# Rearranging the attention slots of a fused attention and MoE kernel

## The chip, the core and the metric

The kernel runs on one core of a Trainium2 chip. The core has a matrix engine (TensorE, "PE" in the profile, with its weight loads shown apart as "PEld"), a vector engine (VectorE, "DVE"), a scalar engine (ScalarE, "ACT"), a general engine (GpSimd, "POOL") and a sync engine ("SP") whose queue issues most of the DMA transfers. Each engine works through its own instructions in program order and waits for the others by semaphores. The metric is the device time of one execution in microseconds (us). Three executions of the kernel before took 841.25 to 842.52 us, median 841.83 us.

## The reference, cut to what matters

```
scores = q @ k.T / 8                           # 4 batches x 8 heads, 576 x 576, head size 64
keep   = scores >= rowmax(scores) - tau
attn   = where(keep, exp(scores - rowmax), 0); attn /= rowsum(attn) + 1e-9
x      = (attn @ v) laid out as [4, 576, 512]
u      = x + mix(x)                            # mix: along the 576 rows, through rank 32 (U, V)
y      = u + relu(u @ w_ch1) @ w_ch2           # 512 -> 2048 -> 512
out    = (sigmoid(conv5(y)) * (y @ w_val)) @ w_out
```

All of it is wanted in fp32 accuracy. The weights U, V, w_ch1, w_ch2, w_val, conv_w and w_out arrive as 64-bit floats and are converted on the chip.

## The kernel before, in words

**Two parts.** Attention and the mixing run first (about the first 335 us of the profile), the dense layers after. In the dense part the matrix engine multiplies back to back; the change does not touch its code.

**Pairs, rows and slots.** Heads are handled in 16 pairs `p`. A pair has nine score tiles `i` = 0 to 8 of 128 queries by 576 keys: tile 0 holds the last 64 queries of both heads, the odd and even tiles after it belong to the first and the second head. The loop over slots (L701) has one score tile in each slot `s` = 9p + i. In the body of a slot VectorE and ScalarE work on tile `s` (row maximum "ns" L443, exponential "e" L457) and on the mask of tile `s`-1 (L468), then the functions put off by `later` run, and last the matrix engine's part is emitted: the scores of tile `s`+1 (L429) first, and then what the table of slots lists for this slot. In what follows "slot i" means the i-th slot of any period of nine.

**What stands in the slots.** A table `AT` says in which slot, counted from the first of pair `p`, each step of the pair is put; numbers over 8 fall into the next pair's slots. `trans_main` transposes the masked tile of two slots earlier (tile xm, L484), `trans_tail` its last 64 keys (xs, L501); `pv` multiplies with v (o, L527 and L538), once for the first two groups of tiles (slot 8) and once for the third (slot 12, which is slot 3 of the next period); `back` transposes the result (b, L548 and L551; slot 14, that is 5); `mix_t`, `mix_u` and `mix_ut` do the mixing (t L577, u L587, ut L597; slots 15 and 18, that is 6 and 0). `prep_T` transposes q, k and their tails for the next pair (tm, L356, and L370). What the matrix engine leaves in PSUM is read by ScalarE and VectorE in the slot after: q's high part on ScalarE (L323) and its low part on VectorE (L329), k likewise (L325, L333), xm to pt (L493), xs to pk (L515), b to ring (L557 on ScalarE, L563 on VectorE), t to t_st (L578, L579).

**Order inside a slot.** `ORDER` ranks the matrix engine's steps, `LATE_ORDER` the functions put off; equal ranks stay in the order in which they were listed, and a put-off function is listed when its step was called.

**Loads and stacks.** q, k and v of coming pairs are loaded two transfers a slot; `AT["lq"]` and `AT["lv"]` are the slots where such a list of loads is begun. `stacks` (slots 4 and 5) copies q and k of the next pair by DMA into the stacked operands `st` of the scores, `tails` (slot 4) does the same for tile 0 on POOL (bd, L401). The stacks and, from pair 4 on, the loads are issued by SP, in program order.

**Weight conversion.** The eight blocks of the first chunk of w_ch1 and w_ch2 are converted beside attention, by generators that move on by one step whenever `work.tick()` runs: in every slot below 18, and then in the slots of `CONVERT_AT`, counted modulo 18. A step is one instruction on ScalarE (L103, L122, L170), VectorE (L105, L108, L112, L116, L126, L172) or POOL (L124, L131, L172).

**PSUM.** Score tiles have two buffers. All other tiles of the matrix engine share four buffers in turn, so that a step may have to wait until the tile of four allocations earlier has been read.

Of the kernel before, what the change touches and what calls it, by code (L numbers as in the profile page):

```python
# [36 lines left out]
def attention_moe_kernel(  # L37
# [24 lines left out]
    NP = B * H // 2  # L62
# [6 lines left out]
    T = B * S  # L69
# [16 lines left out]
    u = const.tile([128, KD, T], F32, name="u")  # L86
# [90 lines left out]
    class Staged:  # L177
# [18 lines left out]


    AT = {
        "pv": (8, 12), "t": 15, "ut": 18, "u": 18, "Tq": 0, "Tk": 1, "Tt": 2, "stA": 4, "bd": 4, "stB": 5,
        "lq": 1, "lv": 5,  # L200
    }

    ORDER = {
        "mix_t": 4, "mix_u": 3, "mix_ut": 5, "next_scores": 0, "prep_T": 5, "pv": 3, "back": 2,
        "trans_main": 1, "trans_tail": 2,
    }
    LATE_ORDER = {
        "T": 1, "n": -1, "nt": -2, "o": -1, "t": 2, "u": 1, "x": -2,
    }

    CONVERT_AT = (0, 1, 4, 9, 10, 13, 16)
    work = Staged(4)

    def scope():
# [11 lines left out]
    def attention(dense_front, dense_mid, dense_back):  # L226
# [18 lines left out]
        bd = [bd_p.tile([128, 2, 128], F32R, name=f"bd{i}") for i in range(2)]  # L245
# [158 lines left out]
        def scores(p, i):  # L404
            d = st8[p]
            s = s_ps.tile([128, 2, 512], F32, tag="s", name="s")
            if i == 0:
                qk, t = d["qk"], bd[p % 2]
                ops = [(t[:, 0, :], qk[:, 1, :]), (t[:, 1, :], qk[:, 1, :]), (t[:, 0, :], qk[:, 2, :])]
            else:  # L410
                c, hh = divmod(i - 1, 2)
                c *= 128
                if p:
                    st = d["st", hh]
                    lhs = st[:, 0, c:c + 128]
                    ops = [(lhs, st[:, 1, :]), (lhs, st[:, 2, :])]
                else:
                    ops = [(d["st", hh][:, m, c:c + 128], d["qk"][:, n, :]) for m in (0, 1) for n in (1, 2)]
                    if hh:
                        for o, n, a in ((s[:, 0], TL, SM), (s[:, 0, TL:], HS - TL, 0), (s[:, 1], HS, HS - TL)):  # L420
                            for m, (lhs, rhs) in enumerate(ops):
                                nc.tensor.matmul(
                                    o[:, 0:n], lhs, rhs[:, a:a + n], start=(m == 0), stop=(m == len(ops) - 1)
                                )
                        d["s", i] = s
                        return
            for n in range(2):
                for m, (lhs, rhs) in enumerate(ops):
                    nc.tensor.matmul(  # L429
                        s[:, n, 0:HS], lhs, rhs[:, n * HS:(n + 1) * HS], start=(m == 0), stop=(m == len(ops) - 1)  # L430
                    )
            d["s", i] = s
# [174 lines left out]
        for hh in range(2):  # L607
            t = st8[0]["st", hh] = st_p.tile([128, 3, S], F32R, tag="st", name="st")
# [57 lines left out]
                nc.gpsimd.tensor_tensor(out=lo, in0=w[a:a + R, o:o + n], in1=f(lo), op=ALU.subtract)  # L666
            done.append(0)

        NS = 9 * NP + AT["u"] - 7
        slots = [[] for _ in range(NS + 1)]  # L670
        def put(s, what, *a):
            slots[s].append((what, a))

        for p in range(NP):
            s0 = 9 * p
            for i in range(9):
                put(s0 + i + 2, trans_main, p, i)
                if i % 2 == 0:
                    put(s0 + i + 2 + (i == 8), trans_tail, p, i)
            put(s0 + AT["pv"][0], pv, p, 0, 1)  # L680
            put(s0 + AT["pv"][1], pv, p, 2)
            put(s0 + AT["pv"][1] + 2, back, p)
            if p + 1 < NP:
                s1 = s0
                put(s1 + AT["Tq"], prep_T, p + 1, "q")
                put(s1 + AT["Tk"], prep_T, p + 1, "k")
                put(s1 + AT["Tt"], prep_T, p + 1, "tail")
                put(s1 + AT["stA"], stacks, p + 1, 0)
                put(s1 + AT["bd"], tails, p + 1)
                put(s1 + AT["stB"], stacks, p + 1, 1)  # L690
            put(s0 + AT["t"], mix_t, p)
            put(s0 + AT["ut"] - (p == NP - 1), mix_ut, p)
            put(s0 + AT["u"] - (p == NP - 1), mix_u, p)
        def next_scores(s):
            scores(*divmod(s + 1, 9))

# [3 lines left out]
        scores(0, 0)  # L700
        for s in range(NS):  # L701
            p, i = divmod(s, 9)
# [6 lines left out]
            def wtick(at):  # L709
                if at == 3 and (s < 18 or s % 18 in CONVERT_AT) or at == 1 and 2 <= s < 8:  # L710
                    work.tick()
# [305 lines left out]
    with tc.manual_schedule():  # L1017
        attention(dense_front(), dense_mid, dense_back)
        dense()
# [30 lines left out]
```

## Time and profile before

| what | value |
|---|---|
| time, median of 3 runs | 841.83 us |
| profiled execution, first to last instruction | 840.1 us |
| PE busy, share of the span | 820.9 us, 98% |
| PEld busy | 692.5 us, 82% |
| DVE busy | 617.3 us, 73% |
| ACT busy | 440.3 us, 52% |
| POOL busy | 239.5 us, 29% |
| PE busy from 60 to 100 us | 38.47 of 40 us |
| DVE busy from 60 to 100 us | 35.01 of 40 us |
| ACT busy from 60 to 100 us | 33.11 of 40 us |

The page of the profile gives the span of the profiled execution and no time of its own around it; the median of the timed runs is 1.73 us above that span. The busy time of PE counts matmuls whose ends are modelled and which overlap, so it hides short waits. The rows of the three stretches at the bottom of the table show that in attention VectorE and ScalarE are nearly as full as the matrix engine.

### The profile page before, as it was taken

The numbers are of one execution on the slowest core, as the hardware profiler recorded it, in microseconds if no ns is written. First come the engines' busy times: TensorE is split into PE (matmuls) and PEld (weight loads), VectorE is DVE, ScalarE is ACT, GpSimd is POOL, SyncE is SP. The second block draws the span as 40 slices with busy tenths as digits, with TensorE's granted clock in tenths as the row PEclk, the third lists the DMA queues.
The fourth block names the chain that finished last, engine by engine and source line by source line (L and its number), as shares of the span: only waits on it lengthen the run. The fifth ranks groups of instructions, "written<-read, shape, count | busy, mean of one in ns | idle before, by whom it ended". The sixth has DMA issues, their size and how long they took to land.

```text
span 840.1 us, 14282 instructions
## 1 busy us (share of the span) xinstructions
PE 820.9 (98%) x5084; PEld 692.5 (82%) x5084; DVE 617.3 (73%) x1309; ACT 440.3 (52%) x894; POOL 239.5 (29%) x329
## 2 busy tenths in 40 slices
PE   8999999999999999999999999999999999999998
PEld 7888877788888888788888888888888888888886
DVE  7988988889989987446883775357753588999740
ACT  5788888888888887422333332133322334445531
POOL 5845533533433432002340252004420143200000
PEclk9999999999999999999999999999999999999999
DMA  5766755665665551002120121002110111001112
GB/s 133 183 134 139 182 129 136 152 156 132 167 160 133 132 114 42 1 0 65 62 77 24 50 98 53 1 1 94 57 51 1 38 64 50 1 1 51 51 50 76
DMA packets 63567, 68.07 MB, mean 81 GB/s; under 512 B 43349, under 2 KB 46821, under 8 KB 63498
## 3 DMA queue, kind: packets, MB, share of 16 engines
q1 hardware_dynamic: 60730, 63.68, 29.4%
q0 software_dynamic: 1424, 3.10, 1.3%
q8 instruction: 41, 0.67, 0.3%
q10 hardware_dynamic: 1344, 0.39, 0.2%
q14 instruction: 28, 0.23, 0.1%
HBM read 35.89 MB, written 4.72 MB: 48 GB/s over the span
## 4 chain that ended last, share of the span: by engine, by line
PE 84%; ACT 6%; DVE 4%; DMA 2%; SPq 2%; issue 2%; POOL 1%; ACTq 0%; DVEq 0%; POOLq 0%
PE a L805 24%; PE c L805 24%; PE o L538 6%; PE s L429 6%; PE v L805 6%; PE p L964 6%; PE xm L484 4%; PE t L577 2%; PE o L527 2%; ACT e L457 2%; ACT pt L493 1%; DVE ns L443 1%; ACT qk L323 1%; DVE e L468 1%; DMA qn<-in_q_dram 1%
## 5 line engine op out<-in xcount | busy, mean ns | idle before, releaser
L805 PE MATMUL a<-us,w 128*128 128x512 f32 (+1 forms) x960 | 202.2, 369 | 0.0
L805 PE MATMUL c<-h,w 128*128 128x512 f32 (+1 forms) x960 | 200.8, 368 | 0.0
L805 PEld LDWEIGHTS a<-us,w 128*128 128x128 f32 x960 | 167.0, 189 | 30.9 <-DVE us L785 0.7
L805 PEld LDWEIGHTS c<-h,w 128*128 128x128 f32 x960 | 167.4, 189 | 30.0
L816 ACT ACTIVATE h<-a 128x512 fp32r<-128x512 f32 (+1 forms) x80 | 44.2, 553 | 187.5 <-PE a L805 187.3
L131 POOL TENSOR_TENSOR wf<-wf,wt 128x512 f32<-128x512 f32 (+2 forms) x43 | 57.5, 1338 | 262.9 <-DVE wt L126 262.9
L817 DVE SCALAR_TENSOR_TENSOR h<-a,h 128x512 fp32r<-128x512 f32 (+1 forms) x80 | 50.8, 636 | 103.9 <-ACT h L816 103.9
L458 POOL TENSOR_TENSOR th<-nm,tau_eff 128x1 f32<-128x1 f32 x135 | 76.8, 570 | 174.8 <-DVE ns L443 173.7
L443 DVE TENSOR_SCALAR_CACHE_REDUCE ns<-s 128x576 f32<-128x576 f32 x144 | 108.1, 751 | 20.2 <-PE s L429 19.7
L468 DVE SCALAR_TENSOR_TENSOR e<-ns,th,e 128x576 f32<-128x576 f32 x144 | 121.2, 842 | 0.5
L457 ACT ACTIVATE e<-ns,nm 128x576 f32<-128x576 f32 x144 | 111.4, 774 | 14.5 <-DVE ns L443 14.0
L429 PE MATMUL s<-st 128*128 128x288 f32 x480 | 94.4, 319 | 2.4 <-DVE ns L443 2.4
L484 PE MATMUL xm<-idn,e 128*128 128x128 f32 x576 | 87.2, 274 | 0.6 <-DVE e L468 0.3
L493 ACT ACTIVATE pt<-xm 128x512 f32<-128x512 f32 x144 | 85.3, 592 | 3.6 <-PE xm L484 0.5
L429 PEld LDWEIGHTS s<-st 128*128 128x128 f32 x480 | 67.9, 189 | 15.2 <-DVE ns L443 6.7
L484 PEld LDWEIGHTS xm<-idn,e 128*128 128x128 f32 x576 | 69.3, 141 | 3.7 <-ACT e L457 1.2
L538 PE MATMUL o<-pt,vt 128*64 128x256 f32 (+1 forms) x768 | 69.8, 331 | 0.0
L538 PEld LDWEIGHTS o<-pt,vt 128*64 128x64 f32 x768 | 41.4, 137 | 24.5 <-issue 8.3
L172 POOL TENSOR_TENSOR w<-wf,w 128x512 fp32r<-128x512 f32 x36 | 53.9, 1513 | 10.1 <-ACT w L170 10.1
L893 DVE SCALAR_TENSOR_TENSOR u<-y,cw,u 128x576 f32<-128x576 f32 x64 | 55.0, 871 | 0.6
L870 DVE TENSOR_TENSOR y<-c,y 128x64 f32<-128x64 f32 (+4 forms) x96 | 39.7, 447 | 21.3 <-PE c L805 21.3
L785 DVE TENSOR_TENSOR us<-u,us 128x1024 fp32r<-128x1024 f32 (+1 forms) x42 | 47.0, 1160 | 10.5 <-ACT us L784 10.5
(122 smaller groups left out, 1035.4 us busy)
## 6 DMA issues: line engine op xcount, KB each, us to landing
raw<-in_moe_w_ch_dram SPq DMA_DIRECT2D x32, 512.0 KB, 3.8
st<-qk SPq DMA_DIRECT2D x30, 256.0 KB, 3.9
st<-qk SPq DMA_DIRECT2D x15, 432.0 KB, 3.9
st<-qk SPq DMA_DIRECT2D x45, 144.0 KB, 4.1
out_dram<-ring SPq DMA_DIRECT2D x17, 256.0 KB, 2.0
st<-qk SPq DMA_DIRECT2D x15, 288.0 KB, 4.8
kn<-in_k_dram SPq DMA_DIRECT2D x28, 128.0 KB, 3.4
qn<-in_q_dram SPq DMA_DIRECT2D x26, 128.0 KB, 3.6
```

The costliest lines, as they stand in the source:

```text
L131: nc.gpsimd.tensor_tensor(out=dst, in0=dst, in1=tf, op=ALU.add)
L172: lo_eng.tensor_tensor(out=lo, in0=w, in1=f(hi), op=ALU.subtract)
L429: nc.tensor.matmul(s[:, n, 0:HS], lhs, rhs[:, n * HS:(n + 1) * HS], start=(m == 0), stop=(m == len(ops) - 1))
L443: nc.vector.tensor_scalar(out=ns.rearrange("p (a b) -> p a b", a=2), in0=s, scalar1=-1.0, scalar2=3.0e38, op0=ALU.mult, op1=ALU.min, accum ...
L457: nc.scalar.activation(out=row(p, i), in_=d["ns", i], func=ACTF.Exp, bias=nm[:, 0:1], scale=-1.0)
L458: (nc.gpsimd if p else nc.vector).tensor_tensor(out=th, in0=nm, in1=tau_eff, op=ALU.add)
L468: nc.vector.scalar_tensor_tensor(out=e, in0=d.pop(("ns", i)), scalar=d.pop(("th", i))[:, 0:1], in1=e, op0=ALU.is_le, op1=ALU.mult, accum_o ...
L484: nc.tensor.transpose(x[:, j * 128:(j + 1) * 128], e[:, c + j * 128:c + (j + 1) * 128], idn)
L493: later(s + 1, 0, lambda: nc.scalar.activation(out=dst, in_=x.rearrange("p (j c) -> p j c", j=4), func=ACTF.Copy), "x")
L538: nc.tensor.matmul(o, lhs, rhs, start=False, stop=stop)
L805: nc.tensor.matmul(ps[:, 0:m1], lhs, rhs, start=(m == 0), stop=(m == len(ops) - 1))
L893: nc.vector.scalar_tensor_tensor(out=g, in0=y[:, e, b, k:k + S], scalar=cw[:, k, e:e + 1], in1=g, op0=ALU.mult, op1=ALU.add)
```

## The change

Numbers in the tables of slots and ranks are changed, with three small edits of the code that reads them. From pair 2 on, the transposes of q move three slots earlier, from slot 0 to slot 6 of the period before (`Tq` -3; for pair 1 they stay in slot 0, `Tq1`). `mix_u` moves from slot 0 to slot 1, except for the last pair. `back` now comes ahead of `trans_main` in its slot, and a `trans_tail` that was listed first does too. t_st comes ahead of what else is put off with it. `tails` moves one slot later. The lists of loads begin one slot earlier. `CONVERT_AT` has five slots of 18 in place of seven.

```diff
     AT = {
-        "pv": (8, 12), "t": 15, "ut": 18, "u": 18, "Tq": 0, "Tk": 1, "Tt": 2, "stA": 4, "bd": 4, "stB": 5,
-        "lq": 1, "lv": 5,
+        "pv": (8, 12), "t": 15, "ut": 18, "u": 19, "Tq": -3, "Tk": 1, "Tt": 2, "stA": 4, "bd": 5, "stB": 5,
+        "lq": 0, "lv": 4, "Tq1": 0,
     }
     ORDER = {
         "mix_t": 4, "mix_u": 3, "mix_ut": 5, "next_scores": 0, "prep_T": 5, "pv": 3, "back": 2,
-        "trans_main": 1, "trans_tail": 2,
+        "trans_main": 2, "trans_tail": 2,
     }
     LATE_ORDER = {
-        "T": 1, "n": -1, "nt": -2, "o": -1, "t": 2, "u": 1, "x": -2,
+        "T": 1, "n": -1, "nt": -2, "o": -1, "t": 0, "u": 1, "x": -2,
     }
-    CONVERT_AT = (0, 1, 4, 9, 10, 13, 16)
+    CONVERT_AT = (0, 1, 6, 9, 16)
...
-        NS = 9 * NP + AT["u"] - 7
-        slots = [[] for _ in range(NS + 1)]
+        NS = 9 * NP + AT["ut"] - 7
+        slots = [[] for _ in range(NS + 2)]
...
             put(s0 + AT["pv"][0], pv, p, 0, 1)
+            end = p == NP - 1
...
-                put(s1 + AT["Tq"], prep_T, p + 1, "q")
+                put(s1 + AT["Tq" if p else "Tq1"], prep_T, p + 1, "q")
...
-            put(s0 + AT["ut"] - (p == NP - 1), mix_ut, p)
-            put(s0 + AT["u"] - (p == NP - 1), mix_u, p)
+            put(s0 + AT["ut"] - end, mix_ut, p)
+            put(s0 + AT["u"] - 2 * end, mix_u, p)
```

The matrix engine, slots 0 to 2 of the period in which pair 2's scores are taken, before (s is a score tile, xm and xs are transposes of a masked tile and of its tail, u and ut the mixing, tm the transposes of q or k):

```order
L587 MATMUL u<-vst,t_st_127 128x512
L589 MATMUL u<-idn,ring 128x128 x4
L597 MATMUL ut<-idn,ring 128x128
L598 MATMUL ut<-vst,t_st_127 128x64
L356 MATMUL tm<-idn,qn 128x128 x4
L429 MATMUL s<-st 128x288 x4
L484 MATMUL xm<-idn,e 128x128 x4
L356 MATMUL tm<-idn,kn 128x128 x4
L429 MATMUL s<-st 128x288 x4
L484 MATMUL xm<-idn,e 128x128 x4
L501 MATMUL xs<-idn,e 128x128
L501 MATMUL xs<-idn,e 64x128
```

The same place on the matrix engine in the changed kernel:

```order
L597 MATMUL ut<-idn,ring 128x128
L598 MATMUL ut<-vst,t_st_127 128x64
L429 MATMUL s<-st 128x288 x4
L484 MATMUL xm<-idn,e 128x128 x4
L587 MATMUL u<-vst,t_st_127 128x512
L589 MATMUL u<-idn,ring 128x128 x4
L356 MATMUL tm<-idn,kn 128x128 x4
L429 MATMUL s<-st 128x288 x4
L501 MATMUL xs<-idn,e 128x128
L484 MATMUL xm<-idn,e 128x128 x4
L501 MATMUL xs<-idn,e 64x128
```

The transposes of q have left slot 0 (they now stand behind t in slot 6), u has gone one slot down beside k, and the tail of tile 8 is transposed ahead of xm.

ScalarE, from the exponential of slot 5 to that of slot 7, before (pt and pk are the copies of xm and xs, rb and ring the result of back, t_st the mixing's first product):

```order
L457 ACTIVATE e<-ns,nm 128x576
L493 ACTIVATE pt<-xm 128x4x128
L555 ACTIVATE rb<-r 64x1
L557 ACTIVATE ring<-b_2024,r 64x64
L557 ACTIVATE ring<-b_2024,rb 64x64
L457 ACTIVATE e<-ns,nm 128x576
L493 ACTIVATE pt<-xm 128x4x128
L515 ACTIVATE pk<-xs 128x128
L578 ACTIVATE t_st_127<-t 128x128
L457 ACTIVATE e<-ns,nm 128x576
```

The same place on ScalarE in the changed kernel (buffers are numbered anew):

```order
L457 ACTIVATE e<-ns,nm 128x576
L555 ACTIVATE rb<-r 64x1
L557 ACTIVATE ring<-b_2007,r 64x64
L557 ACTIVATE ring<-b_2007,rb 64x64
L493 ACTIVATE pt<-xm 128x4x128
L457 ACTIVATE e<-ns,nm 128x576
L493 ACTIVATE pt<-xm 128x4x128
L515 ACTIVATE pk<-xs 128x128
L578 ACTIVATE t_st_127<-t 128x128
L323 ACTIVATE qk<-tm,qscale 128x512
L457 ACTIVATE e<-ns,nm 128x576
```

The three small ring instructions, which the mixing product t waits for, now come ahead of the copy pt, and q's high part (L323) has come in ahead of the exponential of slot 7.

SP's queue, one period of stacks (L383 to L391) and the load of v (vt, vk), before:

```order
L383 DMA st<-qk 64x1728
L384 DMA st<-qk 64x1152
L391 DMA st<-qk 64x576
L387 DMA st<-qk 64x576
L389 DMA st<-qk 64x2x512
L390 DMA st<-qk 64x2x64
L389 DMA st<-qk 64x2x512
L390 DMA st<-qk 64x2x64
L391 DMA st<-qk 64x576
L290 DMA vt_130<-in_v_dram 128x2x256
L296 DMA vk_132<-in_v_dram 64x64 x2
```

The same period in the changed kernel:

```order
L383 DMA st<-qk 64x1728
L384 DMA st<-qk 64x1152
L391 DMA st<-qk 64x576
L290 DMA vt_130<-in_v_dram 128x2x256
L296 DMA vk_132<-in_v_dram 64x64
L387 DMA st<-qk 64x576
L389 DMA st<-qk 64x2x512
L390 DMA st<-qk 64x2x64
L389 DMA st<-qk 64x2x512
L390 DMA st<-qk 64x2x64
L391 DMA st<-qk 64x576
L296 DMA vk_132<-in_v_dram 64x64
```

The load of vt and one vk now stands between the first head's stack and the second head's.

## Rows read from the trace of the kernel before

**Rows 1.** The page's first line.
```profile
span 840.1 us, 14282 instructions
```

**Rows 2.** The chain that ended last, by time: start, length, engine, line, count.
```profile
45.27 1.38 PE t L577 x10
...
291.15 1.35 PE t L577 x10
310.53 1.38 PE t L577 x10
```

**Rows 3.** Waits of PE from 20 to 345 us: total us, times, longest.
```profile
PE o L527 <- ACT pk L515: 4.5, 6, 1.1
PE s L429 <- DVE ns L443: 2.4, 5, 0.8
PE t L577 <- DVE ring L563: 1.9, 4, 0.5
PE t L577 <- ACT ring L557: 1.5, 4, 0.5
```

**Rows 4.** Waits of the weight loads (PEld), same stretch and columns.
```profile
PEld o L527 <- ACT pk L515: 8.5, 16, 1.4
...
PEld t L577 <- ACT ring L557: 6.8, 14, 0.8
PEld s L429 <- DVE ns L443: 6.7, 13, 1.0
```

**Rows 5.** Timeline at a slot 3: start, length, engine, instruction, [idle before <- releaser].
```profile
140.13 0.60 ACT L493 ACTIVATE pt<-xm 128x512 f32<-128x512 f32 x1
...
140.61 0.29 ACT L515 ACTIVATE pk<-xs 128x128 f32<-128x128 f32 x1
...
140.95 0.70 PE L527 MATMUL o<-pk,vk 128*128 128x256 f32 x2 [1.14 <-ACT pk L515]
```

**Rows 6.** Timeline at slots 4 to 6 of the same period.
```profile
143.51 2.57 POOL L124 TENSOR_TENSOR wt<-raw,wt 128x512 f32<-128x512 f32 x2
...
144.97 1.73 DVE L468 SCALAR_TENSOR_TENSOR e<-ns,th,e 128x576 f32<-128x576 f32 x1
...
147.31 0.68 DVE L563 TENSOR_TENSOR ring<-b,r 128x512 f32<-128x512 f32 x1
...
148.14 0.57 PE L577 MATMUL t<-ring,u 128*128 128x128 f32 x3 [0.55 <-DVE ring L563]
```

**Rows 7.** Instructions of DVE by shape, 20 to 335 us: busy, mean ns | idle before.
```profile
L443 DVE TENSOR_SCALAR_CACHE_REDUCE ns<-s 128x576 f32<-128x576 f32 x140 | 105.1, 751 | 20.2 <-PE s L429 19.7
...
L329 DVE SCALAR_TENSOR_TENSOR qk<-tm,qscale,qk 128x512 fp32r<-128x512 f32 x14 | 10.5, 751 | 13.3 <-ACT qk L323 13.1
...
L126 DVE SCALAR_TENSOR_TENSOR wt<-raw,wt 128x512 f32<-128x512 uint32 x5 | 3.4, 674 | 0.0
```

**Rows 8.** Timeline, slots 8 and 9 of one period, with q's copy behind them.
```profile
108.50 0.60 ACT L493 ACTIVATE pt<-xm 128x512 f32<-128x512 f32 x1
...
109.64 0.82 PE L527 MATMUL o<-pk,vk 128*128 128x64 f32 x4
...
113.57 0.76 DVE L443 TENSOR_SCALAR_CACHE_REDUCE ns<-s 128x576 f32<-128x576 f32 x1 [1.83 <-PE s L429]
...
115.99 0.73 ACT L323 ACTIVATE qk<-tm,qscale 128x512 fp32r<-128x512 f32 x1
```

**Rows 9.** Last stack transfer of one period, v's load, its landing, the scores using it.
```profile
129.16 0.71 SPq L391 DMA_DIRECT2D st<-qk  x1
129.96 0.74 SPq L290 DMA_DIRECT2D vt<-in_v_dram  x1
...
DMA to landing us min/median/max: 4.2/4.2/4.2
...
135.79 0.78 PE L429 MATMUL s<-st 128*128 128x288 f32 x4
```

**Rows 10.** Timeline where the dense layers begin.
```profile
336.25 0.69 DVE L785 TENSOR_TENSOR us<-u,us 128x512 fp32r<-128x512 f32 x1 [2.28 <-ACT us L784]
```

## The prediction

> **What bounds the kernel now.** I read first the chain of waits, in order of time, for the starts of the mixing product t, which stands once in every period of nine slots. From 45.27 to 310.53 us lie 13 periods, so a period takes 20.40 us on average. The shortest of them, from 291.15 to 310.53, takes 19.38 us with the same matrix work and little weight conversion [rows 2]. If all 13 ran like it, 13 x 1.02 = 13.3 us would be saved. So the matrix engine bounds attention, and about a twentieth of its time there is waiting.
>
> Where it waits I read from the waits of PE and of its weight loads, which bound it from both sides: a matmul's modelled end covers the first tenths of each wait, so PE's figure is too small, and the weight loads' figure also holds gaps behind which matmuls still ran. Three waits stand out: the second pv of a period (slot 3) for pk, 4.5 to 8.5 us; t (slot 6) for ring, 1.9 + 1.5 = 3.4 to 6.8 us; the scores for a free buffer, that is for ns, 2.4 to 6.7 us [rows 3, 4]. Together 10.3 to 22.0 us, and the 13.3 us of the periods lie between. The dense part I leave as it is.
>
> **Change by parts: pk.** In one slot 3 pk (0.29 us) stands on ScalarE behind pt (0.60 us), and the matrix engine waited 1.14 us there [rows 5]. In the changed order xs is transposed before xm and pk is copied before pt. That takes off up to 0.6 us each time, and q's copy of 0.73 us [rows 8] no longer stands on ScalarE two slots earlier. The longest waits come when a conversion step falls on ScalarE in slot 1; only one of two such slots is left. I take three quarters of the middle of the bounds: 0.75 x 6.5 = 4.9 us (bounds 0 and 8.5).
>
> **t and ring.** ScalarE's ring instructions now stand ahead of a pt, again worth up to 0.6 us, and b is transposed ahead of xm. Where VectorE's ring was last, as in the period of rows 6 (t waited 0.55 us), a mask instruction of 1.73 us stood before it, and beside that ran two POOL instructions of a conversion, 2.57 us in all; it ended 0.6 us after them [rows 6]. They come from the conversion slots 4 and 13, which are slot 4 of their periods; both are gone, and the slot 6 that is new comes behind ring. I take four fifths of the middle: 0.8 x 5.1 = 4.1 us (bounds 0 and 6.8).
>
> **Scores and ns.** VectorE stood idle 13.3 us in 14 instructions before q's low part, because ScalarE's high part came late, and ns of the next scores was queued behind it [rows 7]. With q gone from slots 0 and 1 this blocking goes there, and u's copy, which delayed it, comes a slot later beside k. I take 0.7 x 4.55 = 3.2 us (bounds 0 and 6.7). Sum of the three: 12.2 us.
>
> **What q costs in its new place.** The same transposes, one ScalarE and one VectorE instruction per pair now fall in slots 6 and 7. Counted from the end of q's transposes, ScalarE needs 0.73 us and VectorE 0.75 [rows 7, 8], so the low part is done near 1.6 us, and ns behind it near 2.4. The matrix engine needs that ns only for the scores behind the first pv (slot 8). Before, that pv started at 109.64 and VectorE took up the scores behind it at 113.57, after 1.83 us of idle time [rows 8]; the low part's 0.75 us fits into that. So it is hidden. ScalarE is tighter. The exponential and a pt stand behind q's high part; pv's output needs the buffer which that pt frees. Before, such a pt began at 108.50 and lasted 0.60, and the pv started at 109.64: 0.54 us to spare [rows 8]. q's copy puts 0.73 us ahead of it on ScalarE, and its transposes come ahead of the pv too, about 0.45 us of matrix time: 0.54 - 0.73 + 0.45 = 0.26 us to spare. A conversion step on ScalarE there would use that up. I take 0.5 us in all; bounds: a gain of nothing, a loss of 14 x 0.5 = 7 us.
>
> **Loads and stacks.** vt (0.74 us on SP's queue) and one vk, which I take at 0.6, now stand ahead of the second head's stack, so its last transfer is issued 1.3 us later. Before, it was issued at 129.16 and landed 4.2 us later at 133.36, and the scores that need it started at 135.79: 2.4 us to spare [rows 9]. These scores come about 0.8 us sooner, as u and q have left the slot before, and the stacks start about 0.6 us sooner, since k's low part no longer waits behind q's: 2.4 - 1.3 - 0.8 + 0.6 = 0.9 us to spare. I take 0.3 us for the periods in which it lands late. The earlier start of the lists changes nothing else on SP, and q's loads come long before they are wanted.
>
> **Bounds of attention's end and start.** Fewer conversion slots leave the end of two of the eight weight blocks to the stretch behind the last mask. Two VectorE steps there fall into its 2.28 us of idle time before us [rows 10]; the next one stands between the first and the second us, where the matrix engine takes each as it comes. At the 0.67 us of a row of such a step [rows 7] I take 0.5 us (bounds 0 and 2). At the start, q of pair 2 is written into a buffer that pair 0's scores read until slot 7: ScalarE waits once, 0.4 us (bounds 0 and 1).
>
> **A rule against it.** In rows 6 the mask ran on only when POOL's instructions were over, and then for its usual remainder. The Trainium skill (SBUF — State Buffer, Who interferes with whom) says that VectorE instructions with two SBUF inputs and GpSimd instructions that read SBUF exclude each other, and the later one is blocked entirely. This trace agrees for the long ones. By that rule the copies bd, one slot later, could block the mask ahead of ring in each period; then the term of t would not come, 4.1 us, and the time would be 834.6 us, inside the first rival below. No row here shows a short POOL instruction holding a mask, so the sum goes without it.
>
> **Sum.** 12.2 - 0.5 - 0.3 - 0.5 - 0.4 = 10.5 us; by the periods it would be 13.3 - 1.7 = 11.6. I take 11.3, nearer to the periods, because they hold all waits and the three terms only the named ones. The profiled span of 840.1 us [rows 1] becomes 828.8, and with the 1.73 us by which the median of the runs is longer, 830.5 us.
>
> **Rivals.** First: VectorE or POOL becomes the bound where q went. VectorE has some 18 us of work in a period (35.01 of 40 us in the table of the profile, times 20.40), so a matrix engine at 19.4 us leaves it little slack, and lateness from slot 7 or from bd reaches ring again. Then the terms of t and of ns go, 4.1 + 3.2 = 7.3 us at most, 4.5 us as the middle: 835 us. For it speaks the shift of VectorE's q wait into the slots before ring and pv; against it that pv's idle time of 1.83 us lies right behind.
>
> Second, slower: the second head's stack lands too late. Each us past the 0.9 to spare stops the matrix engine once a period, 14 times. It turns the whole slower by over 0.2% once the stop exceeds (11.3 + 1.7) / 14 = 0.93 us, so once the transfer lands 1.8 us later than reckoned. At 2.4 us late it would cost 14 x 1.5 = 21 us, and 830.5 + 21 = 851.5 us. For it speaks that v's large load now goes over the same DMA engines just ahead; against it that it is one transfer of many.
>
> Third: waits only change their names. Each of the three waits is ended by another, as ScalarE and VectorE are almost full; then 841 us. The order shows that the change does what it says, so that is no rival of its own.
>
> **How the numbers follow.** Two times of this kernel can be told apart from about 0.2%, or 1.7 us. The forecast, 826 to 833.5 us, has 0.58; the first rival, 833.5 to 839, has 0.22; more gain than 826 has 0.05; no change 0.06; slower 0.09. So faster 0.85, same 0.06, slower 0.09. The range from 825 to 839 holds the first two cases and a little of the third: 0.82.
>
> **What would show it.** In the changed profile the starts of t should lie about 19.5 us apart; PE's waits for pk and for ring should be near zero, and VectorE's idle time before q's low part should fall well below 13 us. The conversion's POOL instructions should no longer stand in slot 4. Wrong steps would show as scores that wait for the transfers of st (second rival), o that waits for a pt in slot 8 (q's new place), or t that still waits for VectorE's ring (first rival).

## The result, and the profile after

The changed kernel takes 830.39 us (median of 4 runs, 829.41 to 831.24) against 842.02 for the kernel before (median of 4, 841.25 to 842.52): a ratio of 0.9862, 95% interval 0.9848 to 0.9876, 11.6 us less. The profiled execution, one of the two longer of the four (831.23 us), ran 829.5 us from first to last instruction, 10.6 less than the 840.1 of [rows 1]:

```profile
span 829.5 us, 14295 instructions
```

I divide the span at the first t and at the fourteenth, 13 periods later, as the prediction did. In the chain of waits of the changed kernel the starts of t read (start in us, duration, engine, operation):

```profile
68.51 1.38 PE t L577 x10
87.61 1.38 PE t L577 x10
106.98 1.38 PE t L577 x10
...
279.58 1.38 PE t L577 x10
298.93 1.38 PE t L577 x10
```

Of the 13 steps seven are 19.10 us, five 19.35 to 19.39, and one is 19.25; before, they went from 19.38 to 21.25. The first t stands at 49.11 now (it is not in the chain; the timeline has it). So the three parts of the span are:

| part | before | after | gain |
|---|---|---|---|
| start to the first t | 45.27 | 49.11 | -3.84 |
| 13 periods | 265.26 | 249.81 | 15.45 |
| 14th t to the end | 529.57 | 530.58 | -1.01 |

Two tables of busy time, of the kernel before and of the changed one, over just these 13 periods (window; its length, and the busy time of PE, its weight loads, VectorE, ScalarE and POOL, each with its count of instructions; granted clock; DMA share; GB/s):

```profile
45.27:310.53 265.26, 254.41 (x2132) 213.80 (x2132) 234.25 (x613) 217.65 (x502) 106.22 (x190) 1.00 0.61 141
```
```profile
49.11:298.92 249.81, 248.93 (x2132) 213.86 (x2132) 227.37 (x602) 213.44 (x499) 103.92 (x188) 1.00 0.63 150
```

The same 2132 matrix instructions at the same granted clock of 1.00. The matrix engine stood idle 10.85 us before and 0.88 now; another 5.5 us went from its busy time, which is where modelled ends had covered the first tenths of each wait. What it still waits for, from 20 to 345 us, first by PE and then four rows by the weight loads (waiter, releaser, us in total, times, longest):

```profile
PE s L429 <- POOL bd L401: 3.0, 1, 3.0
PE s L422 <- DVE ns L443: 1.0, 1, 1.0
PE xm L484 <- DVE e L468: 0.7, 2, 0.4
PE a L806 <- DVE us L786: 0.6, 1, 0.6
PE o L527 <- ACT pk L515: 0.5, 1, 0.5
```
```profile
PEld t L577 <- ACT pt L493: 4.3, 15, 0.3
PEld s L429 <- DVE ns L443: 4.0, 11, 0.4
...
PEld o L527 <- ACT pk L515: 0.9, 1, 0.9
PEld o L527 <- ACT pt L493: 0.8, 4, 0.2
```

Of the waits of [rows 3, 4] that for pk is left once (8.5 to 0.9 us by the weight loads), none for ring, and that for ns falls from 6.7 to 4.0. (The 0.3 us before each of the 15 t, now put down to pt, stands in the shortest periods too. So does the gap of 0.4 us before scores that makes up the 4.0: in the period from 203.03 us, which takes 19.10, it stands twice, once put down to ns and once to r, L475.) Two rows are new, for bd and for us: they are the losses at the two ends.

**The start.** POOL in the kernel before and in the changed one, in order of time (start, duration, operation):

```profile
24.29 1.60 POOL L401 TENSOR_SCALAR bd<-qk 64x64 fp32r<-64x64 f32 x4
...
26.67 4.66 POOL L666 TENSOR_TENSOR vst<-wf,vst 32x352 fp32r<-32x352 f32 x4
```
```profile
25.86 4.53 POOL L666 TENSOR_TENSOR vst<-wf,vst 32x352 fp32r<-32x352 f32 x4
30.49 1.61 POOL L401 TENSOR_SCALAR bd<-qk 64x64 fp32r<-64x64 f32 x4
```

One slot later in the program, bd of pair 1 stands behind the four vst instructions of the setup, 4.53 us, and the scores that read it wait:

```profile
31.83 1.89 PE L429 MATMUL s<-qk,bd 128*128 128x288 f32 x6 [2.97 <-POOL bd L401]
```

**The end.** Conversion now reaches into the stretch where the operands us of the dense layers are made. Its VectorE steps stand where the prediction put them: two (L126, L112) before the first us, one (L116) between the first and the second. But a POOL step of the same conversion runs beside the first us, which takes 1.34 us on VectorE where it took 0.69 [rows 10], and a waits 0.57 us behind it (start, duration, engine, operation):

```profile
323.57 1.67 POOL L131 TENSOR_TENSOR wf<-wf,wt 128x512 f32<-128x512 f32 x1 [2.05 <-DVE wt L126]
```
```profile
324.46 1.34 DVE L786 TENSOR_TENSOR us<-u,us 128x512 fp32r<-128x512 f32 x1 [0.37 <-ACT us L785]
```
```profile
325.85 3.06 PE L806 MATMUL a<-us,w 128*128 128x512 f32 x11 [0.57 <-DVE us L786]
```

### The profile page after: what moved, and what is told of

Its sections match the earlier page's. It is cut to its first block, busy times and chain, and to the rows that moved or that the text cites. A ratio compares the mean times of both kernels' runs of the same rounds, so it can differ in the third digit from the quotient of the medians.

```text
span 829.5 us, 14295 instructions
## 1 busy us (share of the span) xinstructions
PE 815.3 (98%) x5084; PEld 691.9 (83%) x5084; DVE 616.2 (74%) x1309; ACT 437.4 (53%) x894; POOL 240.3 (29%) x329
## 4 chain that ended last, share of the span: by engine, by line
PE 90%; ACT 4%; DMA 2%; POOL 2%; DVE 1%; issue 1%; SPq 0%; ACTq 0%; DVEq 0%; POOLq 0%
PE c L806 24%; PE a L806 24%; PE s L429 8%; PE o L538 8%; PE v L806 6%; PE p L965 6%; PE xm L484 6%; PE t L577 2%; PE o L527 2%; ACT pt L493 1%; PE tm L356 1%; ACT e L457 1%; PE u L589 1%; PE xs L501 1%; DMA st<-qk 1%
## 5 line engine op out<-in xcount | busy, mean ns | idle before, releaser
L458 POOL TENSOR_TENSOR th<-nm,tau_eff 128x1 f32<-128x1 f32 x135 | 80.7, 598 | 165.9 <-DVE ns L443 164.5
L468 DVE SCALAR_TENSOR_TENSOR e<-ns,th,e 128x576 f32<-128x576 f32 x144 | 119.5, 830 | 0.7 <-ACT e L457 0.5
L457 ACT ACTIVATE e<-ns,nm 128x576 f32<-128x576 f32 x144 | 111.5, 774 | 13.3 <-DVE ns L443 12.9
L538 PEld LDWEIGHTS o<-pt,vt 128*64 128x64 f32 x768 | 41.4, 137 | 24.5 <-issue 10.6
```

The costliest lines, as they stand in the source:

```text
L457: nc.scalar.activation(out=row(p, i), in_=d["ns", i], func=ACTF.Exp, bias=nm[:, 0:1], scale=-1.0)
L458: (nc.gpsimd if p else nc.vector).tensor_tensor(out=th, in0=nm, in1=tau_eff, op=ALU.add)
L468: nc.vector.scalar_tensor_tensor(out=e, in0=d.pop(("ns", i)), scalar=d.pop(("th", i))[:, 0:1], in1=e, op0=ALU.is_le, op1=ALU.mult, accum_o ...
L538: nc.tensor.matmul(o, lhs, rhs, start=False, stop=stop)
```

## The experiments

Periods are always counted as above, from the first t to the fourteenth, and waits of PE or its weight loads are those from 20 to 345 us. Runs of one group share the runs of the kernel before: 841.63 us for e1 to e4, 841.65 for e5 to e8, 841.58 for e9 to e11.

**What the start and the end cost (e1 to e4).** The first undoes the later slot of bd for the first pair alone:

```diff
-                put(s1 + AT["bd"], tails, p + 1)
+                put(s1 + AT["bd"] - (not p), tails, p + 1)
```

> The changed kernel, with the copies bd of pair 1 alone put back to slot 4 (all other pairs keep slot 5). Theory A (the start costs 3.8 us because POOL runs pair 1's bd behind four long instructions L666 and the matrix engine waits 3.0 us for it): the wait PE s <- POOL bd goes to zero, the first t starts near 45.9 us (49.1 in the changed kernel, 45.3 before), and the time falls by 3.2 us to about 827.2 us. Theory B (the start is bound by VectorE's and ScalarE's work in the first slots, and bd was only the last to come): another wait takes its place between 28 and 49 us, the first t moves by under 1 us, and the time stays within 1 us of 830.4. Both: the spacing of t afterwards stays 19.1 to 19.4 us.

Measured: 827.59 us (826.28 to 828.18), ratio 0.9829 (0.9814 to 0.9844). The row for bd is gone from the waits, which now begin

```profile
PE s L422 <- DVE ns L443: 1.0, 1, 1.0
PE xm L484 <- DVE e L468: 0.8, 2, 0.4
PE a L806 <- DVE us L786: 0.6, 1, 0.6
PE o L527 <- ACT pk L515: 0.5, 1, 0.5
```

The first t starts at 46.11 and the 13 periods take 249.78 us, as in the changed kernel. So theory A stands. Behind the vst instructions bd cost 3.0 us up to the first t in these two executions, and 2.8 us by the medians, where 3.2 was expected. This version has the lowest median of all that ran, though its interval overlaps that of e3 below. (The start also differs from execution to execution by where the granted clock falls; see the last section.)

The second gives one conversion slot back, `CONVERT_AT = (0, 1, 6, 9, 12, 16)`, and the third does both edits:

> The changed kernel with a sixth conversion slot, 12 (slot 3 of the odd pairs, beside the second pv), so that all eight weight blocks are converted before the last mask. Theory A (the end costs about 1 us because conversion steps stand between the us instructions): the wait PE a <- DVE us of 0.6 us goes, the stretch from the last t of slot 6 before the dense layers to the end is 1.0 us shorter, and the periods keep 19.1 to 19.4 us, so the time falls by about 1.0 us to 829.4. Theory B (each conversion slot in the periods costs what it saves at the end): periods with the new slot get longer by 0.3 us or more, 7 times 0.3 = 2 us, and the time rises to about 831.5.

> Both edits together (bd of pair 1 in slot 4, a sixth conversion slot 12). Theory A: the two savings add, 830.4 - 3.2 - 1.0 = 826.2 us. Theory B of either edit: 827 to 831 us.

Measured: 830.52 us (830.49 to 832.29), ratio 0.9873 (0.9856 to 0.9889), and 828.37 (827.81 to 828.87), ratio 0.9840 (0.9826 to 0.9855). The wait of a for us goes as expected, and e2 takes 1.2 us less from the 15th t to the end. But periods of 19.47, 19.85 and 20.11 us appear, the 13 take 251.32 and 251.36 us, 1.5 more, and the 14th takes 18.87 instead of 18.12. What a conversion step saves at the end it costs in the periods, so nothing is won.

The fourth puts the starts of the loads back, `"lq": 1, "lv": 5`:

> The changed kernel with the lists of loads begun at their old slots (lq 1, lv 5), so that vt and vk again follow both stacks on SP. Theory A (the second head's stack lands in time in either order, as no wait of the scores for st shows): same time within 0.5 us, 830.4. Theory B (the earlier loads are part of the gain): up to 2 us slower. Theory C (v's load ahead of the second stack costs hidden waits): up to 2 us faster. The wait for bd at the start should be a little different, as POOL's vt load moves behind L666: at most 0.7 us earlier.

Measured: 830.12 us (829.14 to 831.12), ratio 0.9861 (0.9847 to 0.9876); 13 periods in 249.82 us. The place of the loads is indifferent to the periods. The wait for bd is 1.2 us here instead of 3.0, but that is only in part the place of v's load. bd ends at 31.32 us on POOL, against 32.10 in the changed kernel. And in e2, whose loads stand as in the changed kernel, the wait is shorter still, 0.7 us: in both runs the granted clock was 0.50 just before (23.2 to 26.6 us in e4, 20.7 to 27.5 in e2) and the matrix engine came later to the scores that read bd (its wait begins at 29.83 us in e4 and 30.67 in e2, against 28.86).

**Which part of the change gives what (e5 to e8).** Three runs make one part alone on the kernel before, the fourth takes one from the changed kernel:

```diff
e5  -        "trans_main": 1, "trans_tail": 2,
    +        "trans_main": 2, "trans_tail": 2,
    -        ... "t": 2, "u": 1, "x": -2,
    +        ... "t": 0, "u": 1, "x": -2,
e6  -    CONVERT_AT = (0, 1, 4, 9, 10, 13, 16)
    +    CONVERT_AT = (0, 1, 6, 9, 16)
e7  -        ... "u": 18, "Tq": 0, ... "lq": 1,
    +        ... "u": 19, "Tq": -3, ... "lq": 0, "Tq1": 0,
e8  the changed kernel with "u": 18, "Tq": 0, "Tq1": 0
```

> The kernel before with the order alone: xs transposed ahead of xm, and ring ahead of pt. Theory A (the three parts take off different waits, and their gains add): the waits for pk fall from 4.5 us (PE's figure) to about 1.5, those of t for ScalarE's ring go, those of t for VectorE's ring stay; 13 periods shorter by about 5 us, time near 837. Theory B (one part carries nearly all, the move of q): here 840 to 842, the waits for pk stay above 3 us.

> The kernel before with five conversion slots instead of seven. Theory A: the waits of t for VectorE's ring go from 1.9 us to near 0 and pk's two longest go; 13 periods shorter by about 4 us, of which the end of attention takes 1 back: near 838.5. Theory B: 841 to 842.

> The kernel before with q's transposes three slots sooner and the mixing product u one slot later; bd and the load of v stay where they were. Theory A: the waits of the scores for ns go (2.4 us of PE's, 6.7 of the weight loads'), VectorE's idle time before q's low part falls from 13.3 us to about 4; 13 periods shorter by about 6 us, the waits for pk and ring stay; the first t comes 0.5 us later at most: time near 836. Theory B: near 832, with the waits for pk and ring gone too.

> The changed kernel with q's transposes and u put back to their old slots. Theory A: the scores wait for ns again, some 6 us longer than the changed kernel, near 836, with the waits for pk and ring still near zero. Theory B: nearly the whole gain goes, 839 to 842.

Measured, with e9 and e10 from below (pk and t by PE, t's waits for ring or pt together; ns by the weight loads):

| kernel | us, ratio (interval) | 13 periods | pk | t | ns |
|---|---|---|---|---|---|
| before | | 265.26 | 4.5 | 3.4 | 6.7 |
| e5 order | 838.59, 0.9965 (0.9952 to 0.9978) | 262.62 | 1.2 | 1.3 | 8.6 |
| e6 conversion | 833.39, 0.9902 (0.9888 to 0.9917) | 256.40 | 1.0 | 0 | 6.9 |
| e7 q and u | 837.31, 0.9948 (0.9933 to 0.9962) | 260.97 | 4.6 | 2.8 | 1.9 |
| e8 all but q and u | 836.94, 0.9942 (0.9926 to 0.9959) | 254.84 | 0.5 | 0 | 7.3 |
| after | 830.39, 0.9862 (0.9848 to 0.9876) | 249.81 | 0.5 | 0 | 4.0 |
| e9 slot 10 | 836.72, 0.9942 (0.9926 to 0.9959) | 259.61 | 0.6 | 1.5 | 8.4 |
| e10 slots 4, 13 | 838.43, 0.9962 (0.9947 to 0.9977) | 260.07 | 1.9 | 0 | 8.6 |

Theory A holds in its main point: the gains in the periods are 2.64, 8.86 and 4.29 us, 15.79 together, against 15.45 for all at once, and no part alone carries nearly all. (Order and conversion overlap a little: alone they sum to 11.50, and e8, which has both, gives 10.42. The later slot of bd in the pairs after the first was not tried apart.) It misses the shares: I expected 5, 4 and 6. In e5 the waits for pk and for ring fell further than expected, and yet only half of the time came. Two weight-load rows of e5 show where the rest may have gone, since ns is 6.7 us in [rows 4]:

```profile
PEld s L429 <- DVE ns L443: 8.6, 19, 0.8
...
PEld o L527 <- ACT pk L515: 3.5, 7, 0.9
```

This fits a matrix engine that, relieved at pk and ring, came sooner to scores whose ns was still late. In e7 it is the other way round:

```profile
PEld o L527 <- ACT pk L515: 7.3, 11, 1.0
PEld t L577 <- ACT ring L557: 6.3, 14, 0.8
...
PEld s L429 <- DVE ns L443: 1.9, 6, 0.4
```

q's move takes the waits for ns away and leaves those for pk and ring. VectorE's idle time before q's low part, 13.3 us in [rows 7], fell to 9.3 in e7, where about 4 was expected, and in the changed kernel to this (idle time last, with its releaser):

```profile
L329 DVE SCALAR_TENSOR_TENSOR qk<-tm,qscale,qk 128x512 fp32r<-128x512 f32 x14 | 10.5, 750 | 4.3 <-ACT qk L323 3.3 <-DMA st<-qk 0.5
L333 DVE TENSOR_TENSOR qk<-tm,qk 128x512 fp32r<-128x512 f32 x14 | 9.7, 690 | 4.2 <-ACT qk L325 4.0
```

Part of it has moved: before k's low part (L333) VectorE stood idle 1.2 us in the kernel before.

**Which conversion slots (e9, e10).** e9 leaves out slot 10 alone, `(0, 1, 4, 9, 13, 16)`; e10 slots 4 and 13, `(0, 1, 9, 10, 16)`.

> The kernel before without conversion slot 10, the slot 1 of every second period, and nothing else. Theory A (each conversion slot delays what stands behind it there): the waits for pk fall from 4.5 us (PE's figure) to 2 or less, those of t for VectorE's ring stay at about 1.9; time 838 to 839. Theory B (the conversion slots cost by their load on the engines, wherever they stand): waits for pk and for ring both fall by about a third; time near 838.9, a third of the 8.3 us that all three slots gave.

> The kernel before without conversion slots 4 and 13, the slot 4 of every period. Theory A: the waits of t for VectorE's ring go, from 1.9 us to 0.5 or less, while those for pk stay above 3.5; time 836 to 838. Theory B: both fall by about two thirds; time near 836.1.

Measured: 836.72 and 838.43 us. Neither theory is right. First e9, then e10:

```profile
PE s L429 <- DVE ns L443: 2.1, 4, 0.5
PE t L577 <- ACT ring L557: 1.2, 3, 0.5
PE s L422 <- DVE ns L443: 1.0, 1, 1.0
PE o L527 <- ACT pk L515: 0.6, 1, 0.6
PE t L577 <- DVE ring L563: 0.3, 1, 0.3
```
```profile
PE s L429 <- DVE ns L443: 2.2, 5, 0.6
PE o L527 <- ACT pk L515: 1.9, 4, 0.6
```

Each slot takes off the wait that stands behind it, as A says (pk from 4.5 to 0.6 in e9; ring to nothing in e10), and most of the other as well (VectorE's ring from 1.9 to 0.3 in e9; pk from 4.5 to 1.9 in e10), which is neither A's "stays" nor B's equal shares. This fits lateness that is carried from slot to slot. In the periods e9 and e10 give 5.65 and 5.19 us, 10.8 together, while e6, which leaves out all three slots and adds slot 6, gives 8.86. Which of the two takes the 2 us, the overlap or the slot added, was not tried apart.

**The slower rival (e11).** The version of e1, with the second head's stack behind more loads on SP's queue:

```diff
-        ... "stB": 5,
-        "lq": 0, ...
+        ... "stB": 7,
+        "lq": 3, ...
```

> The best version so far (the changed kernel with bd early) with the second head's stack issued behind more loads on SP's queue: k's and the tails' loads of the pair after next now stand ahead of it, besides v's, about 2.5 us of issue time more in each period. Theory A (the second rival's mechanism, about 1 us to spare): the scores of the second tile wait for st by 0.5 to 1.8 us in each of 13 or 14 periods; time 835 to 852, the starts of t 20 to 21 us apart. Theory B (there is more to spare than reckoned): within 1 us of 827.6, no wait for st.

Measured: 850.49 us (848.43 to 852.64), ratio 1.0107 (1.0086 to 1.0127); the 13 periods take 270.87 us, 21.1 more than in e1. The scores of the second tile, in three periods:

```profile
54.62 0.77 PE L429 MATMUL s<-st 128*128 128x288 f32 x4 [0.60 <-DMA st<-qk]
94.89 0.77 PE L429 MATMUL s<-st 128*128 128x288 f32 x4 [1.60 <-DMA st<-qk]
117.25 0.77 PE L429 MATMUL s<-st 128*128 128x288 f32 x4 [3.10 <-DMA st<-qk]
```

Seven such waits sum to 8.8 us. One of 4.76 us at the same tile (223.56) is put down to a load of q, but the stack's last transfer but one (L390), issued at 217.72, landed only 5.4 us later, so it was the stack there too. Where the trace tells the landing of the last transfer, in nine of the 13 periods, these scores start 0.1 to 0.3 us behind it. The stack's last transfer is issued 5.89 us after t here (135.57 against 129.68), and 3.45 in e1 (126.51 against 123.06): 2.44 us later, and theory A stands, though the waits go up to 4.76 us where it had 1.8. The mechanism is real; the change only stops short of it. In the changed kernel the last transfer, its landing and the scores that need it are

```profile
129.67 0.73 SPq L391 DMA_DIRECT2D st<-qk  x1
...
DMA to landing us min/median/max: 2.8/2.8/2.8
...
134.62 0.78 PE L429 MATMUL s<-st 128*128 128x288 f32 x4
```

It lands 2.8 us after its issue, where [rows 9] had 4.2, and that leaves 134.62 - 129.67 - 2.8 = 2.15 us to spare. Over the ten of the 13 periods in which the trace tells the landing, 0.8 to 2.4 us are to spare; the least is in the period from 106.98 us, where the transfer takes 3.8 us to land.

## Why the prediction was right, and where its steps were not

The forecast was 830.5 us; it came to 830.39. The mechanism was right; that the number came so close is luck, since two errors cancelled. For the periods the working had 12.2 - 0.5 - 0.3 = 11.4 us, and they gave 15.45, 4.05 more. For the end and the start it had 0.5 + 0.4 = 0.9 us, and they cost 4.85, 3.95 more.

**What bounds the kernel.** Right that it is the matrix engine. But the best period of [rows 2], 19.38 us, was taken as the floor for all, and it was none: seven periods now take 19.10, and the gain of 15.45 us goes beyond the 13.3 that this floor allowed.

**pk, t and ring.** The terms came to 4.9 + 4.1 = 9.0 us. The run that has all of the change but q and u (e8) gives 265.26 - 254.84 = 10.4, 1.4 more. They can't be told apart further: e9 and e10 show that a conversion slot delays both.

**Scores and ns.** This term was too small. Taken at 3.2 less 0.5 for q's new place, 2.7 us net; q's move measures 254.84 - 249.81 = 5.0 us on top of the other parts, and 4.3 alone. The 6.7 us of [rows 4], taken as the upper bound of the wait, were not one: with the other waits reduced the same wait grows to 7.3 to 8.6 us (e5, e8, e9, e10). Taking seven tenths of the middle of a wait seen beside others undervalued it. For the same reason the third rival, waits that only change names, was half true for each part alone (e5 most), and false for all together, as the parts reach all three waits. The waits of xm for the exponential (1.5 us, 7 times, by the weight loads of e8), which no term counted, are gone in the changed kernel as well.

**q's new place.** Right in kind, and at the place that was named. ScalarE, from q's copy to the pt that pv's buffer waits for, in a period of 19.37 us and in one of 19.10:

```profile
127.98 0.69 ACT L323 ACTIVATE qk<-tm,qscale 128x512 fp32r<-128x512 f32 x1 [0.21 <-DMA vt<-in_v_dram]
128.57 0.77 ACT L457 ACTIVATE e<-ns,nm 128x576 f32<-128x576 f32 x1
129.24 0.67 ACT L103 ACTIVATE wt<-raw 128x512 f32<-128x512 f32 x1
129.80 0.59 ACT L493 ACTIVATE pt<-xm 128x512 f32<-128x512 f32 x1
```
```profile
147.35 0.69 ACT L323 ACTIVATE qk<-tm,qscale 128x512 fp32r<-128x512 f32 x1 [0.21 <-DMA vt<-in_v_dram]
147.94 0.77 ACT L457 ACTIVATE e<-ns,nm 128x576 f32<-128x576 f32 x1
148.61 0.59 ACT L493 ACTIVATE pt<-xm 128x512 f32<-128x512 f32 x1
```

A conversion step (L103, L122 or L170) stands ahead of that pt in the five periods of 19.35 to 19.39 us and in no other, and in four of the five o waits 0.2 us for pt by the weight loads. Five times 0.27 is some 1.3 us, where 0.5 was taken and 7 was the bound.

**The rule against it.** The Trainium skill (SBUF — State Buffer, Who interferes with whom) would have let bd, one slot later, block the mask in each period. It did not come to that test: in all 13 periods of the changed kernel bd lies between two masks, as after 203.03 us, where one mask runs from 219.66 to 220.47 us, bd from 220.48 to 221.57, and the next mask from 221.68. t waits for no ring, so the rule changed nothing here; whether a short POOL copy can hold a mask is not shown.

**Loads and stacks.** 0.9 us to spare was reckoned; 0.8 is the least that the trace shows, most periods have 1.2 us or more, and no scores wait for st. 0.3 us was taken and nothing was lost. The second rival's price came out, 21 us for 2.4 us later against 21.1 lost in the periods of e11, but partly by luck: it had 14 stops of 1.5 us, and e11 has eight named stops of 0.5 to 4.8 us, 13.6 in all.

**The end.** 0.5 us was taken (bounds 0 and 2), 1.0 measured, in the stretch that was named. The working priced a VectorE step; the wait that came stands behind a us that ran beside a POOL step, which it did not count.

**The start.** The step that failed: 0.4 us was taken (bounds 0 and 1), 3.84 measured. The wait that it named, ScalarE's for q's buffer, is there: q's copy at 28.52 us comes after 0.80 us of idle time that is put down to a score matmul. It costs about what was taken. In the executions whose granted clock stayed at 1.00 from 18 to 45 us the first t starts at 44.38 us (e10, up to there the program of before), 44.96 (e7, q and u moved) and 44.70 (e3, the change with bd early). What came on top was bd on POOL. The working treated bd's later slot only where the mask might meet it, in the periods, and did not look at what stands ahead of bd on POOL's own queue in the first pair, four instructions of 4.66 us in all. They stand there in the program of before already, as the rows above show.

## What to carry to other kernels

A step moved by a slot is moved past whatever its engine's queue holds in that slot, and the first and last rounds hold other things than the steady one; look at each. When several waits stand in one period, size them together from the best period, since what one releases another can take up until the last of them is gone; and look for what the best period itself still waits for, as here it allowed 13.3 us and 15.45 came. Reckon a transfer's margin to the use behind it, not the number of its instructions, and over several periods, since the time to land varies: here 0.8 us at the least was enough, and 2.4 us later cost 21.

## What the hardware showed besides

The granted clock of the matrix engine fell to half, 1.2 of 2.4 GHz, for some stretches behind waits: in the changed kernel behind its wait of 2.97 us, and in the kernel before behind waits for ns of 1.39 and 0.96 us that ended at 18.5 and 21.9 us (same columns as the windows above):

```profile
31.80:34.80 3.00, 2.97 (x13) 2.93 (x14) 1.04 (x3) 0.19 (x1) 1.50 (x4) 0.50 0.71 264
```
```profile
22.70:26.00 3.30, 3.30 (x16) 3.22 (x16) 3.27 (x8) 2.43 (x6) 3.08 (x7) 0.50 0.95 194
```

In e11 it was 0.66 and 0.50 behind the waits of 3.10 and 4.76 us, and stayed 1.00 behind those of 0.60 and 1.60. But the two waits of the kernel before stand in the changed kernel too (1.40 and 0.96 us), where the clock stayed at 1.00 until 31.7 us, and in e3, e7 and e10, where it was 1.00 from 18 to 45 us; so what decides at the start stays open. In the stretch of the changed kernel six score matmuls took 1.89 us, where six of the same kind take 1.04 at 128.65 us of the same profile. So a wait behind which the clock falls costs more than its length. The 21.1 us of e11 exceed the 13.6 of the waits named for it by 7.5; how much of that is the clock was not measured apart.
